# Attention values by key block in 64x64 quarters, and a Newton chain in PSUM

## The chip, the cores and the metric

The kernel runs on one core of a Trainium2 chip. The core has a matrix engine, TensorE (PE), whose weight loads are listed as PEld; VectorE (DVE), ScalarE (ACT) and GpSimd (POOL) for elementwise work; and SyncE (SP), which issues most transfers. SBUF and PSUM are its on-chip memories of 128 partitions. PE writes its results into PSUM, which has eight banks of 512 fp32 columns per partition. The metric is device time in microseconds (us) of one execution, the median of several runs.

## The reference

A windowed causal attention is followed by a gated expert. With 8 batches, 8 heads, 576 positions and 64 values per head:

```python
scores = scale * np.matmul(q, k.transpose(0, 1, 3, 2))
mask = (rel >= 0) & (rel < window)                 # window 64
attn = np.exp(scores - max); attn = attn / (sum + 1e-09)
out = np.matmul(attn, v)                           # (B, H, S, D)

x = out.transpose(0, 2, 1, 3).reshape(B * S, H * D)     # 4608 tokens of 512
xn = x / sqrt(mean(x * x) + 1e-06) * rms_g
g, val = xn @ w_gate, xn @ w_val                   # 512 x 1536
y = (g * sigmoid(g) * val) @ w_out                 # 1536 x 512
```

With a window of 64, a query sees only keys of its own block of 64 and of the block before it. So a key block j takes part in query blocks j and j+1 alone.

## The kernel before

**Batches, pairs, blocks.** Attention works on a pair of heads at a time: four pairs per batch, `n = 4 * b + hp`, 32 in all, each with nine blocks of 64 positions (`NBLK`). The expert works on nine tiles of 512 tokens: it takes its input as a high and a low half in fp16, and each product is three matmuls. Tiles 1 and 2 are done with plain products (`group_in`, `chunk_out`); tiles 3 to 8 with seven products on quarters of the operands instead of eight (`seventh`, L1213, and for the second layer `outer_unit`, L1093), whose weights are prepared beforehand (`prepare`, `prepare_out`) and loaded again from memory as `sevens` and `outer`. PE's unit of such a product is 12 matmuls of 128x256.

**An order written by hand.** After the start (batches 0 and 1, the widening of the weights, tile 0), `rest_of_tiles` (L1285) goes through slots. A slot is about one unit of PE (plain groups count two). `at_slot` enters a piece of work with a due time in slots, and all that is due by a slot is written into the program before the slot's unit. Each engine runs its instructions in this order. The due times of attention are in `WHEN` (one table for batches 2 and 3, one for 4 to 7), counted from the start of tile b - 1: `tile_start` gives 0, 72 and 144 for batches 2, 3 and 4, then 63 more for each. `PREPARE` and `PREPARE_OUT` hold start and spacing of the preparations.

**Banks.** In this stage all eight banks of PSUM go through one list (`any_bank`, L97): the first of the list is taken, and `done_with` puts a bank at its end when the last reader has been written into the program. PE waits on the chip until that reader has run. In tiles 3 to 8 a product a1 keeps its bank over the units 0 to 12 of its chunk, a5 from unit 2 to 8, a2 for one unit; chunks start seven slots apart; `times` (L1169 to L1173) frees a bank some two to three slots after its last unit (`DONE`, `TANH`, `TIMES`). Scores take three banks: s0 for block 0, then one for each head; the masks free s0 first.

**Attention of a pair in batches 2 to 7.** `load_kv` (L340) loads keys and values in one transfer. The values lie with even blocks in partitions 0 to 63 and odd blocks in 64 to 127; `even` holds block 2u above block 2u - 1. A query block j needs key blocks j - 1 and j under one another: for even j that is not what `even` has, so two further transfers (L363, L364) load a shifted copy, `odd`. `scores_of_pair` (L430) multiplies queries by keys in quarters (`quarter`, L408): 64 rows of one head, 64 columns of one block, up to 128 keys; the four (head, parity) quarters follow one another in the order of `QUARTERS`. The mask (DVE, L425), exponential (ACT, L428) and scaling (POOL, L383) follow; then the weights are turned by a way through memory (L391, L397) and a transpose of 32x32 blocks (DVE, L400, L401). `values` (L606) then does `attention_values` (L536) in two halves of five and four query blocks, the second half due 0.4 slot after the first: for each block and head one matmul of 128 rows (two key blocks), 64 columns and 64 queries into a bank `xp`, and one copy by ACT (L623) into `xb`. `squares` (ACT) and `add` (POOL, for the last pair DVE, L647) collect the sum of squares. They are due 1.5 and 2.2 slots after the values, and use the pair's keys as scratch.

**Roots.** `inverse_roots` (L765) sums the squares over partitions with matmuls into a bank `tot` (five columns) and `inverse_root` (L783) makes 1/sqrt from them on DVE: a line into m (L785), a first guess from the bits of m (L786), then three Newton steps of three instructions (L790 to L792) on the SBUF tile `rm` (m, r, w). `broadcast` (L794) spreads r with matmuls (`rb`, L801), and `normalise` scales and halves the tile's input.

Of the kernel before, what the change touches and what calls it, by code (L numbers as in the profile page):

```python
# [15 lines left out]
F32 = mybir.dt.float32  # L16
# [6 lines left out]
ALU = mybir.AluOpType  # L23
# [20 lines left out]
WHEN = [{'scores': [-13.59, -5.21, 8, 18.26], 'values': [15.58, 22.47, 33.48, 46.85], 'queries': [-6, -6, -6, -6], 'keys': [-6.13, -8.13, -6, -5.32], 'turn': [23.21, 22, 22, 22.22], 'back': [15.94, 16, 16, 15.39], 'away': [12.41, 12.5, 12.08, 13.25], 'mask': [0.36, 0.57], 'exp': [1.39, 0.67], 'sum': 9.7, 'scale': 10, 'roots': 50.0, 'first': [52.21, 0.85], 'second': [58.92, 1.15]}, {'scores': [-15.06, -4.11, 7.56, 21.23], 'values': [16.7, 22, 34.61, 46.18], 'queries': [-4.86, -8.35, -5.85, -6], 'keys': [-6, -6, -5.27, -6], 'turn': [20.48, 23.66, 23.92, 21.6], 'back': [16, 16, 16, 15.9], 'away': [12.5, 12.5, 11.38, 12.5], 'mask': [0.38, 0.71], 'exp': [1.49, 0.69], 'sum': 9.7, 'scale': 10, 'roots': 50.5, 'first': [53.82, 0.85], 'second': [59.57, 0.85]}]  # L44
# [5 lines left out]
PREPARE_OUT = [(117.64, 0.7), (127.0, 0.7), (135.37, 0.7), (145.0, 0.7), (154.0, 0.7), (163.0, 0.7)]  # L50
HALVES = 0.4
DONE = 1.05
TANH = 0.88
# [1 line left out]
SUMS_AT = 0.78  # L55
FREED = 1.1
STREAM = (20, 38)
PREPARE = [(3.0, 0.9), (11.29, 0.9), (23.04, 0.9), (31.8, 1.05), (41.96, 1.07), (51.0, 0.9), (60.6, 0.77), (69.87, 0.9), (79.8, 1.08), (87.32, 0.8), (99.16, 1.41), (113.5, 1.05)]
ST = 2 * NBLK * P - 32
NRB = B  # L60
S1 = [-2, 1, 3, 6, 10, 12.5, 15.5, 19]
# [12 lines left out]
def tile_window_attention_moe(  # L74
# [265 lines left out]
    def load_kv(n):  # L340

        if n == 3:
            kvt = wk.tile([P, 2, NKD, TT], F16, tag="xn", name=f"kv_{n}")
            kvt = kvt.rearrange("p a b c -> p (a b c)").bitcast(F32)[:, : S + NBLK * P]
        else:
            kvt = wk.tile([P, S + NBLK * P], F32, tag="kv", name=f"kv_{n}", bufs=NKV)
        if n < NPAIR:
            nc.sync.dma_start(out=kvt[:, :S], in_=kv[n, :, :S])
        else:
            nc.sync.dma_start(out=kvt[:, : S + NKT * P], in_=kv[n])  # L350
        even = kvt[:, S : S + NKT * P].rearrange("p (u c) -> p u c", c=P)
        odd = kvt[:, S + NKT * P :].rearrange("p (u c) -> p u c", c=P)

        def values_in():
            nc.sync.dma_start(out=kvt[:, S : S + NKT * P], in_=kv[n, :, S : S + NKT * P])
            nc.vector.tensor_copy(odd[0:D], even[0:D, : NKT - 1, :])
            nc.vector.tensor_copy(odd[D:P], even[D:P, 1:, :])

        if n < NPAIR:
            later[n] = values_in  # L360
        else:
            src = kv[n, :, S : S + NKT * P].rearrange("p (u c) -> p u c", c=P)
# [42 lines left out]
    def units(g, h):  # L405
        return [1 + 4 * g + 2 * h + i for i in range(2)] + ([0] if g == h == 0 else [])
# [110 lines left out]
    def weights_to_keys(n, g, ps):  # L517
# [15 lines left out]
            pts.append(pt)  # L533
        return pts

    def attention_values(n, g, at, vv, xp):  # L536

        xp = xp or x_bank(f"xp_{n}_{g}")
        for c, j in enumerate(range(5) if g == 0 else range(5, 9)):
            rows = slice(0, P if j else D)  # L540
            for h in range(2):
                hd = slice(h * D, (h + 1) * D)
                i, par = divmod(j - 1 - 4 * g, 2)
                w = at(1 + 4 * g + 2 * h + i, rows, par) if j else at(0, rows, h)
                o = xp[hd, c * D : (c + 1) * D]
                nc.tensor.matmul(  # L546
                    o if len(w.shape) == 2 else o.rearrange("p (a b) -> p a b", b=32),
                    lhsT=vv[j][rows, hd],
                    rhs=w,
                    start=True,  # L550
                    stop=True,
                    skip_group_check=True,
                )
        return xp
# [3 lines left out]
    def attention(b):  # L558
# [21 lines left out]
        def moves(hp):  # L580
            n = b * NPAIR + hp

            def turned():
                p, m, _ = whole.pop(n)
                turn(p, m)
                soft[hp, 0] = soft[hp, 1] = p
# [15 lines left out]

        def to_keys(hp, g):
            soft[hp, g] = weights_to_keys(b * NPAIR + hp, g, soft[hp, g])

        def values(hp, g, xp=None):  # L606
            n = b * NPAIR + hp
            assert b < TB or chain[n] == 4 + g
            chain[n] = 5 + g
            vv = pairs[hp][1]  # L610
            p = soft.pop((hp, g))
            if isinstance(p, list):
                place = {u: p[h][:, i, :] for h in range(2) for i, u in enumerate(units(g, h))}
                at = lambda u, rows, a: place[u][rows, a * D : (a + 1) * D]
            else:
                at = lambda u, rows, a: p[rows, 2 * a : 2 * a + 2, slot(u), :]
# [24 lines left out]
        def add(hp):  # L641
            ssq = norm["ssq"]
            chain["add", b] = chain.get(("add", b), 0) + 1
            assert chain[b * NPAIR + hp] == 6 and chain["squares", b] >= chain["add", b]
            if hp:
                e = nc.vector if (E('ADD', 'ppvppv')[3 * b + hp - 1] == 'v' if b < 2 else hp == NPAIR - 1) else nc.gpsimd
                e.tensor_tensor(ssq, ssq, pairs[hp][0], ALU.add)  # L647
# [10 lines left out]
            return normalise(b, norm["x"], norm["r"], piece)  # L658

        if b >= TB:  # L660
            return load_queries, load_keys, score_pair, moves, values, squares, add, roots, normal_parts
        return load_queries, load_keys, score, to_keys, values, roots, normal

    def attention_events(b, start, pace, tags):
# [25 lines left out]
            timed.sort(key=lambda e: e[:2])  # L690

    def attention_slots(b):
        load_queries, load_keys, score_pair, moves, values, squares, add, roots, normal_parts = attention(b)
        t0 = tile_start(b - 1)

        def all_of(hp, when):
# [11 lines left out]
        for hp in range(NPAIR):  # L708
# [74 lines left out]
    def inverse_root(m, r, w, squares):  # L783
# [3 lines left out]
            r.bitcast(I32), m.bitcast(I32), -0.5, RSQRT_SEED, ALU.mult, ALU.add  # L787
        )
        for _ in range(3):
            nc.vector.tensor_tensor(w, r, r, ALU.mult)  # L790
            nc.vector.scalar_tensor_tensor(w, w, -0.5, m, ALU.mult, ALU.mult)
            nc.vector.scalar_tensor_tensor(r, w, 1.5, r, ALU.add, ALU.mult)  # L792

    def broadcast(b, r, a, z):  # L794
# [722 lines left out]
```

## Time and profile before

| what | value |
|---|---|
| runs | 991.19, 991.77, 991.29 us; median 991.29 |
| profiled execution | 990.32 us, its span 988.5 |
| granted PE clock, mean of the span | 0.983 |
| moved by DMA | 193.89 MB, mean 196 GB/s |
| instructions | 22548 |

The profile is of one execution. It has the busy time of each engine, groups of instructions by line, what ended the idle time before an instruction (in brackets, with an arrow to the engine, tile and line it waited for), a timeline, and windows with busy time, granted PE clock (1.00 is full) and DMA share. A row of the timeline is start, length, engine, line, operation, output and inputs, shape and how many were merged. A fp32 matmul appears as two records. PE's records overlap at their ends, since matmuls are pipelined, so the cost of a piece on PE is better read from one start to the next. In rows of waits the numbers are the sum in us, how often, and the longest.

### The profile page before, as it was taken

To read this page: it belongs to the slowest core of one execution; us is meant where nothing else is said; L and a number is where in the kernel's file an instruction comes from. 1 tells how busy PE (TensorE), PEld (TensorE's weight loads), DVE (VectorE), ACT (ScalarE), POOL (GpSimd) and SP (SyncE) were. 2 spreads that over 40 slices of the span, in tenths; PEclk is the share of its full clock that TensorE was granted. 3 is DMA by queue.
4 is the path that set the end of the run, shared out by engine and by line. 5 is a ranking of instruction groups with operands and counts; after the bars stand their busy time and mean duration, and the time that the engine had idled before them with its cause. 6 is when DMAs were issued, how large, how long until landed. Compare 5 with 4: busy or idle time off the path is not lost.

```text
span 988.5 us, 22548 instructions
## 1 busy us (share of the span) xinstructions
PE 950.5 (96%) x8465; PEld 693.4 (70%) x8465; DVE 663.8 (67%) x1839; ACT 545.6 (55%) x1404; POOL 420.3 (43%) x481
## 2 busy tenths in 40 slices
PE   7779989999999999989999999999999999999998
PEld 5544544544444454467888888888888898888887
DVE  5678968248776766869865776778577846743761
ACT  5567887245435543356755674676477536642652
POOL 3335643134424542344635454545345525440440
PEclk9989989999999999999999999999999999999999
DMA  7525661226545875477758976887598736645641
GB/s 289 188 86 183 208 216 37 70 86 181 132 132 162 220 222 171 140 240 265 228 212 255 326 241 206 288 295 263 187 299 299 224 103 231 203 143 194 223 156 43
DMA packets 106653, 193.89 MB, mean 196 GB/s; under 512 B 28208, under 2 KB 65072, under 8 KB 106544
## 3 DMA queue, kind: packets, MB, share of 16 engines
q1 hardware_dynamic: 105968, 191.27, 60.7%
q8 instruction: 66, 1.08, 0.4%
q10 hardware_dynamic: 576, 1.18, 0.3%
q14 instruction: 43, 0.35, 0.1%
HBM read 154.67 MB, written 37.75 MB: 195 GB/s over the span
## 4 chain that ended last, share of the span: by engine, by line
PE 88%; DMA 4%; DVE 4%; ACT 3%; issue 1%; SPq 1%; ACTq 0%; DVEq 0%
PE a L1141 32%; PE o L1084 15%; PE xp L546 5%; PE sc L412 4%; PE pv L888 3%; PE po L888 3%; PE po L890 3%; PE pg L888 3%; PE po L889 3%; PE pv L890 3%; PE pv L889 3%; PE pg L890 3%; PE pg L889 3%; DMA kv<-kv 2%; DMA wt<-sevens 1%; PE tr L527 1%
## 5 line engine op out<-in xcount | busy, mean ns | idle before, releaser
L1141 PEld LDWEIGHTS <-wt 128*128 128x128 f16 x3024 | 294.2, 98 | 37.9 <-issue 0.8
L1141 PE MATMUL a<-xn,wt 128*128 128x256 f16 x1728 | 203.1, 273 | 0.0
L1210 POOL TENSOR_TENSOR wt<-u,wt 128x512 f16<-128x512 f32 x72 | 66.2, 920 | 152.6 <-ACT wt L1208 98.6
L1141 PE MATMUL a<-wt,wt 128*128 128x256 f16 x1044 | 127.1, 273 | 0.0
L1175 ACT ACTIVATE th<-a,hsc 128x256 f32<-128x256 f32 x144 | 67.9, 472 | 94.4 <-DVE a L1239 75.7
L1210 POOL TENSOR_TENSOR h<-th,h 128x512 f16<-128x512 f32 x72 | 85.5, 1189 | 45.8 <-ACT h L1208 44.1
L1084 PE MATMUL o<-wt,h 128*128 128x256 f16 x864 | 101.1, 273 | 0.0
L428 ACT ACTIVATE pm<-pm,st 128x128 f32<-128x128 f32 (+1 forms) x216 | 83.8, 390 | 19.7 <-DVE st L425 19.5
L1084 PEld LDWEIGHTS <-h 128*128 128x128 f16 x864 | 84.1, 98 | 10.6 <-issue 1.0
L1170 DVE SCALAR_TENSOR_TENSOR th<-th,a 128x256 f32<-128x256 f32 x144 | 59.4, 412 | 34.5 <-ACT th L1175 32.7
L1239 DVE TENSOR_TENSOR a<-a,s 128x512 f32<-128x512 f32 x72 | 50.2, 697 | 46.1 <-PE a L1141 43.6
L383 POOL TENSOR_TENSOR pm<-pm,st 128x512 f32<-128x512 f32 (+1 forms) x72 | 60.5, 866 | 41.9 <-DVE st L461 20.5
L1084 PEld LDWEIGHTS <-wt 128*128 128x128 f16 x648 | 63.5, 99 | 7.2
L941 POOL TENSOR_TENSOR h<-th,h 128x512 f16<-128x512 f32 x30 | 38.2, 1273 | 65.2 <-ACT h L940 55.4
L1171 DVE SCALAR_TENSOR_TENSOR th<-a,th 128x256 f32<-128x256 f32 x144 | 61.1, 424 | 5.0
L412 PE MATMUL sc<-kv,q 64*64 64x128 f32 (+1 forms) x1056 | 55.7, 297 | 8.3 <-DMA q<-q 4.9
L425 DVE CUSTOM_DVE_ANT_0 pm<-sc,blocked 128x128 f32<-128x128 f32 x192 | 49.3, 283 | 15.4 <-PE sc L412 15.3
L888 PE MATMUL pg<-xn,wt 128*128 128x512 f16 x144 | 55.0, 382 | 2.3 <-ACT wt L249 1.5
L888 PE MATMUL pv<-xn,wt 128*128 128x512 f16 x144 | 55.8, 388 | 0.7 <-DVE th L936 0.7
L890 PE MATMUL pv<-xn,wt 128*128 128x512 f16 x144 | 55.9, 388 | 0.0
L889 PE MATMUL pv<-xn,wt 128*128 128x512 f16 x144 | 55.8, 387 | 0.0
L888 PEld LDWEIGHTS <-wt 128*128 128x128 f16 x296 | 29.2, 99 | 36.8 <-issue 2.4
(197 smaller groups left out, 1940.1 us busy)
## 6 DMA issues: line engine op xcount, KB each, us to landing
wt<-sevens SPq DMA_DIRECT2D x72, 512.0 KB, 5.3
wt<-sevens SPq DMA_DIRECT2D x36, 768.0 KB, 5.0
wt<-outer SPq DMA_DIRECT2D x24, 768.0 KB, 4.5
kv<-kv SPq DMA_DIRECT2D x28, 608.0 KB, 5.5
via<-pm SPq DMA_DIRECT2D x96, 144.0 KB, 3.4
pm<-via SPq DMA_DIRECT2D x24, 576.0 KB, 4.4
q<-q SPq DMA_DIRECT2D x28, 288.0 KB, 5.1
kv<-kv SPq DMA_DIRECT2D x56, 128.0 KB, 6.0
```

The source lines that it names most:

```text
L383: nc.gpsimd.tensor_tensor(p[:, :ks, us, :], p[:, :ks, us, :], r, ALU.mult)
L412: nc.tensor.matmul(out.rearrange("p (n c) -> p n c", c=D), lhsT=qt[hd, j * D : (j + 1) * D], rhs=halves[hd, :1, :] if j == 0 else halves[h ...
L428: nc.scalar.activation(part, part, AF.Exp, bias=low, scale=-1.0, accum_out=total)
L888: nc.tensor.matmul(acc, lhsT=lh, rhs=rh, start=first, stop=False)
L889: nc.tensor.matmul(acc, lhsT=lh, rhs=rl, start=False, stop=False)
L890: nc.tensor.matmul(acc, lhsT=ll, rhs=rh, start=False, stop=last)
L1084: nc.tensor.matmul(acc[:, sub * HT : (sub + 1) * HT], lhsT=l[:, x, sub * P : (sub + 1) * P], rhs=r[:, y, :], start=first and c == cs[0] an ...
L1141: nc.tensor.matmul(acc[:, i * HT : (i + 1) * HT], lhsT=ws[l][:, kt, :], rhs=b[:, m, kt, :], start=at_start, stop=kt == 1 and j == 2, skip_ ...
L1170: nc.vector.scalar_tensor_tensor(cols, cols, 1.0, acc[:, :HT], ALU.add, ALU.mult)
L1171: nc.vector.scalar_tensor_tensor(cols, acc[:, HT:], 2.0**-42, cols, ALU.mult, ALU.mult)
L1175: nc.scalar.activation(cols, acc[:, :HT], AF.Tanh, scale=th_scale[:, c : c + 1])
L1210: nc.gpsimd.tensor_tensor(lo, src, hi, ALU.subtract)
```

## The change

For pairs of batches 2 to 7 values are computed by key block. Key block m (64 rows: the lower or upper half of the partitions by its parity) is multiplied by the weights of query blocks m and m + 1 at once, for each head: sixteen matmuls of 64 rows, 64 columns and 128 queries and two of 64 queries (block 8), in the order of `QUARTERS`. Even and odd key blocks go to separate banks: x0 has query blocks 0 to 5 of the even ones, x1 blocks 6 to 8, x2 blocks 1 to 8 of the odd ones. The three banks are taken together. `take` copies x0 and x1 (ACT, 384 and 192 columns) and adds x2 (DVE, 512 columns), 0.9, 1.0 and 1.3 slots after the values; squares and additions follow at 2.2 and 3. The shifted copy is no longer loaded for these pairs. The weights are in one tile for the whole pair, as before.

In the roots, m and w are now columns of the bank `tot`, which is released after the chain; the Newton step multiplies m by r first, then by r again. This holds for all eight batches.

Due times change too (before, after):

| entry | before | after |
|---|---|---|
| batches 2 and 3, values | 15.58, 22.47, 33.48, 46.85 | 12.69, 20.07, 33.48, 43.56 |
| back | 15.94, 16, 16, 15.39 | 16.42, 16.48, 16.48, 15.87 |
| away, third pair | 12.08 | 13.8 |
| exp, sum, scale | 1.39, 9.7, 10 | 1.34, 10.6, 10.9 |
| roots; first piece | 50.0; 52.21 by 0.85 | 50.9; 54.11 by 0.93 |
| batches 4 to 7, scores, third pair | 7.56 | 7.51 |
| values, fourth pair | 46.18 | 46.28 |
| turn, second pair | 23.66 | 23.78 |
| first piece; second piece | 53.82; 59.57 | 54.15; 57.1 |
| PREPARE, 1st; 6th; 7th; 8th | 3.0; 51.0 by 0.9; by 0.77; by 0.9 | 2.8; 51.89 by 1.11; by 0.98; by 0.88 |
| PREPARE_OUT, 5th | 154.0 by 0.7 | 154.12 by 0.82 |

```diff
+TAKEN = [0.9, 1.0, 1.3]
+SQUARED = [2.2, 3]
...
         if n < NPAIR:
             later[n] = values_in
-        else:
+        elif n < TB * NPAIR:
             src = kv[n, :, S : S + NKT * P].rearrange("p (u c) -> p u c", c=P)
             nc.sync.dma_start(out=odd[0:D], in_=src[0:D, : NKT - 1, :])
             nc.sync.dma_start(out=odd[D:P], in_=src[D:P, 1:, :])
+        else:
+            return kvt[:, :S], [even[(j % 2) * D : (j % 2 + 1) * D, (j + 1) // 2, :] for j in range(NBLK)]
...
+    def values_by_keys(n, p, vv):
+
+        xs = [x_bank(f"x{i}_{n}") for i in range(3)]
+
+        def product(m, h):
+            x, j0 = (xs[2], 1) if m % 2 else (xs[0], 0) if m < 6 else (xs[1], 6)
+            rows, hd = slice((m % 2) * D, (m % 2 + 1) * D), slice(h * D, (h + 1) * D)
+            js = range(m, min(m + 2, NBLK))
+            w = []
+            for j in js:
+                i, par = divmod(j - 1, 2)
+                u, a = (1 + 4 * (i // 2) + 2 * h + i % 2, par) if j else (0, h)
+                w.append(p[rows, 2 * a : 2 * a + 2, slot(u), :])
+            step = w[-1].offset - w[0].offset
+            nc.tensor.matmul(
+                x[hd, (m - j0) * D : (m - j0 + len(w)) * D].rearrange("p (x a b) -> p x a b", x=len(w), b=32),
+                lhsT=vv[m][:, hd],
+                rhs=bass.AP(tensor=p.tensor, offset=w[0].offset, ap=[w[0].ap[0], [step, len(w)], *w[0].ap[1:]]),
+                start=True,
+                stop=True,
+                skip_group_check=True,
+            )
+
+        for m in range(0, NBLK - 1, 2):
+            for h, odd in QUARTERS:
+                product(m + odd, h)
+        for h in range(2):
+            product(NBLK - 1, h)
+        return xs
...
+        def weigh_values(hp):
+            n = b * NPAIR + hp
+            sums[hp] = values_by_keys(n, soft.pop((hp, 0)), pairs[hp][1])
+
+        def take(hp, i):
+            n = b * NPAIR + hp
+            if hp == i == 0:
+                new_sums()
+            x = norm["x"][:, hp, :]
+            if i < 2:
+                a, z = ((0, 6 * D), (6 * D, S))[i]
+                nc.scalar.copy(x[:, a:z], sums[hp][i][:, : z - a])
+            else:
+                nc.vector.tensor_tensor(x[:, D:], x[:, D:], sums[hp][i], ALU.add)
+            done_with(f"x{i}_{n}")
...
-            at_slot(v, partial(values, hp, 0))
-            at_slot(v + 0.4, partial(values, hp, 1))
-            at_slot(v + 1.5, partial(squares, hp))
-            at_slot(v + 2.2, partial(add, hp))
+            at_slot(v, partial(weigh_values, hp))
+            for i in range(3):
+                at_slot(v + TAKEN[i], partial(take, hp, i))
+            at_slot(v + SQUARED[0], partial(squares, hp))
+            at_slot(v + SQUARED[1], partial(add, hp))
...
-        rm = wk.tile([P, 3, nst], F32, tag="rm", name=f"rm_{b}", bufs=1)
-        m, r, w = (rm[:, i, :] for i in range(3))
+        r = wk.tile([P, nst], F32, tag="rm", name=f"rm_{b}", bufs=1)
+        m, w = (tot[:, 8 * i : 8 * i + nst] for i in range(1, 3))
...
         for _ in range(3):
-            nc.vector.tensor_tensor(w, r, r, ALU.mult)
-            nc.vector.scalar_tensor_tensor(w, w, -0.5, m, ALU.mult, ALU.mult)
+            nc.vector.tensor_tensor(w, m, r, ALU.mult)
+            nc.vector.scalar_tensor_tensor(w, w, -0.5, r, ALU.mult, ALU.mult)
             nc.vector.scalar_tensor_tensor(r, w, 1.5, r, ALU.add, ALU.mult)
```

More of the change, by code (lines that the diff above doesn't have):

```diff
@@ L43 @@
 LV0 = [2.6, 2.6, 2.6, 2.6, 2.6, 2.6, 2.6, 2.6]
-WHEN = [{'scores': [-13.59, -5.21, 8, 18.26], 'values': [15.58, 22.47, 33.48, 46.85], 'queries': [-6, -6, -6, -6], 'keys': [-6.13, -8.13, -6, -5.32], 'turn': [23.21, 22, 22, 22.22], 'back': [15.94, 16, 16, 15.39], 'away': [12.41, 12.5, 12.08, 13.25], 'mask': [0.36, 0.57], 'exp': [1.39, 0.67], 'sum': 9.7, 'scale': 10, 'roots': 50.0, 'first': [52.21, 0.85], 'second': [58.92, 1.15]}, {'scores': [-15.06, -4.11, 7.56, 21.23], 'values': [16.7, 22, 34.61, 46.18], 'queries': [-4.86, -8.35, -5.85, -6], 'keys': [-6, -6, -5.27, -6], 'turn': [20.48, 23.66, 23.92, 21.6], 'back': [16, 16, 16, 15.9], 'away': [12.5, 12.5, 11.38, 12.5], 'mask': [0.38, 0.71], 'exp': [1.49, 0.69], 'sum': 9.7, 'scale': 10, 'roots': 50.5, 'first': [53.82, 0.85], 'second': [59.57, 0.85]}]
+WHEN = [{'scores': [-13.59, -5.21, 8, 18.26], 'values': [12.69, 20.07, 33.48, 43.56], 'queries': [-6, -6, -6, -6], 'keys': [-6.13, -8.13, -6, -5.32], 'turn': [23.21, 22, 22, 22.22], 'back': [16.42, 16.48, 16.48, 15.87], 'away': [12.41, 12.5, 13.8, 13.25], 'mask': [0.36, 0.57], 'exp': [1.34, 0.67], 'sum': 10.6, 'scale': 10.9, 'roots': 50.9, 'first': [54.11, 0.93], 'second': [58.92, 1.15]}, {'scores': [-15.06, -4.11, 7.51, 21.23], 'values': [16.7, 22, 34.61, 46.28], 'queries': [-4.86, -8.35, -5.85, -6], 'keys': [-6, -6, -5.27, -6], 'turn': [20.48, 23.78, 23.92, 21.6], 'back': [16, 16, 16, 15.9], 'away': [12.5, 12.5, 11.38, 12.5], 'mask': [0.38, 0.71], 'exp': [1.49, 0.69], 'sum': 9.7, 'scale': 10, 'roots': 50.5, 'first': [54.15, 0.85], 'second': [57.1, 0.85]}]
 FIRST7 = 3
@@ L49 @@
 OUT_ORDER = ((1, 0), (1, 1), (5, 0), (5, 1), (2, 0), (2, 1), (1, 2), (5, 2)) + tuple((p, u) for p in (6, 3, 7) for u in range(3)) + ((2, 2), (4, 0), (4, 1), (4, 2))
-PREPARE_OUT = [(117.64, 0.7), (127.0, 0.7), (135.37, 0.7), (145.0, 0.7), (154.0, 0.7), (163.0, 0.7)]
+PREPARE_OUT = [(117.64, 0.7), (127.0, 0.7), (135.37, 0.7), (145.0, 0.7), (154.12, 0.82), (163.0, 0.7)]
+TAKEN = [0.9, 1.0, 1.3]
+SQUARED = [2.2, 3]
 HALVES = 0.4
@@ L57 @@
 STREAM = (20, 38)
-PREPARE = [(3.0, 0.9), (11.29, 0.9), (23.04, 0.9), (31.8, 1.05), (41.96, 1.07), (51.0, 0.9), (60.6, 0.77), (69.87, 0.9), (79.8, 1.08), (87.32, 0.8), (99.16, 1.41), (113.5, 1.05)]
+PREPARE = [(2.8, 0.9), (11.29, 0.9), (23.04, 0.9), (31.8, 1.05), (41.96, 1.07), (51.89, 1.11), (60.6, 0.98), (69.87, 0.88), (79.8, 1.08), (87.32, 0.8), (99.16, 1.41), (113.5, 1.05)]
 ST = 2 * NBLK * P - 32
@@ L585, in turned @@
                 turn(p, m)
-                soft[hp, 0] = soft[hp, 1] = p
+                soft[hp, 0] = p
             when = WHEN[b > FIRST7]
@@ L604, in to_keys, with new_sums @@
             soft[hp, g] = weights_to_keys(b * NPAIR + hp, g, soft[hp, g])
+        sums = {}
+        def new_sums():
+            norm["x"] = wk.tile([P, NPAIR, S], F32, tag="xb", name=f"xb_{b}", bufs=1)
+            norm["ssq"] = wk.tile([P, S], F32, tag="ssq", name=f"ssq_{b}", bufs=1)
+        def weigh_values(hp):
+            n = b * NPAIR + hp
+            assert chain[n] == 4
+            chain[n] = 5
+            sums[hp] = values_by_keys(n, soft.pop((hp, 0)), pairs[hp][1])
+        def take(hp, i):
+            n = b * NPAIR + hp
+            assert chain[n] == 5 + i
+            chain[n] = 6 + i
+            if hp == i == 0:
[7 more added lines that the diff above has]
+            done_with(f"x{i}_{n}")
         def values(hp, g, xp=None):
             n = b * NPAIR + hp
-            assert b < TB or chain[n] == 4 + g
-            chain[n] = 5 + g
             vv = pairs[hp][1]
             p = soft.pop((hp, g))
[L612 to L616, printed above, removed]
+            place = {u: p[h][:, i, :] for h in range(2) for i, u in enumerate(units(g, h))}
+            at = lambda u, rows, a: place[u][rows, a * D : (a + 1) * D]
             xp = attention_values(n, g, at, vv, xp)
             if hp == g == 0:
-                norm["x"] = wk.tile([P, NPAIR, S], F32, tag="xb", name=f"xb_{b}", bufs=1)
-                norm["ssq"] = wk.tile([P, S], F32, tag="ssq", name=f"ssq_{b}", bufs=1)
+                new_sums()
             xb, ssq = norm["x"], norm["ssq"]
@@ L624, in values @@
             done_with(f"xp_{n}_{g}")
-            if g == 0:
-                return
-            if b < TB:
+            if g:
                 squares(hp)
@@ L643, in add @@
             chain["add", b] = chain.get(("add", b), 0) + 1
-            assert chain[b * NPAIR + hp] == 6 and chain["squares", b] >= chain["add", b]
+            assert (b < TB or chain[b * NPAIR + hp] == 8) and chain["squares", b] >= chain["add", b]
             if hp:
@@ L660, in attention @@
         if b >= TB:
-            return load_queries, load_keys, score_pair, moves, values, squares, add, roots, normal_parts
+            return load_queries, load_keys, score_pair, moves, weigh_values, take, squares, add, roots, normal_parts
         return load_queries, load_keys, score, to_keys, values, roots, normal
@@ L692, in attention_slots @@
     def attention_slots(b):
-        load_queries, load_keys, score_pair, moves, values, squares, add, roots, normal_parts = attention(b)
+        load_queries, load_keys, score_pair, moves, weigh_values, take, squares, add, roots, normal_parts = attention(b)
         t0 = tile_start(b - 1)
```

## The prediction

> **What bounds the kernel now.** I read the page first, then what TensorE (PE) waits for once the attention of batch 2 has begun, then PE's timeline piece by piece.
>
> ```profile
> PE 950.5 (96%) x8465; PEld 693.4 (70%) x8465; DVE 663.8 (67%) x1839; ACT 545.6 (55%) x1404; POOL 420.3 (43%) x481
> ```
>
> PE is busy for 96% of the span and no other engine for more than 67%. The second view groups PE's waits from 220 us to the end: total, number, longest.
>
> ```profile
> PE s L412 <- DMA kv<-kv: 2.9, 2, 2.5
> PE tot L769 <- DVE ssq L647: 2.6, 2, 2.1
> PE xp L546 <- DVE th L1171: 2.3, 1, 2.3
> ```
>
> That is 7.8 us of waiting in 768 us. So in this stage the time is what PE's own pieces cost, and an edit counts if it shortens a piece, removes one of these three waits, or makes a new one. The reader should see that the first wait is for keys and the other two are for VectorE (DVE).
>
> The profiled execution took 990.32 us (span 988.5); the median of the runs is 991.29. I sum against 990.32 and add the 0.97 at the end.
>
> **Values: what a pair costs now, and in quarters.** Rows of PE's timeline: start, length, line, shape, count.
>
> ```profile
> 503.33 1.41 PE L546 MATMUL xp<-pm,kv 64*64 64x64 f32 x36
> 504.67 1.48 PE L1141 MATMUL a<-xn,wt 128*128 128x256 f16 x12
> 506.09 0.27 PE L412 MATMUL s<-kv,q 64*64 64x64 f32 x2
> ...
> 507.23 0.94 PE L1084 MATMUL o<-wt,h 128*128 128x256 f16 x7
> ```
>
> Lengths overlap by a tail, so the cost of a piece is the difference of two starts. A pair's values in one go cost 504.67 - 503.33 = 1.34. A pair's scores cost 507.23 - 506.09 = 1.14. Both are 36 records (18 fp32 matmuls, two records each). The scores are sixteen matmuls of 64x64x128 and two of 64x64x64 over the four quarters of the array, with banks separated by the row half; the new values are the same sixteen and two, also with a bank for each row half. So I price the new values at the scores' row: 1.14. Their right side comes in runs of 32 floats where the scores' comes in runs of 64; the values' runs are of 32 today too.
>
> In batches 4 to 7 most pairs are not in one go: the second half is due 0.4 slot after the first, and where a slot begins between them a product unit comes in between.
>
> ```profile
> 532.85 1.47 PE L1141 MATMUL a<-wt,wt 128*128 128x256 f16 x12
> 534.16 1.47 PE L1141 MATMUL a<-xn,wt 128*128 128x256 f16 x12
> ...
> 554.40 0.95 PE L546 MATMUL xp<-pm,kv 64*64 64x64 f32 x20
> 555.28 1.48 PE L1141 MATMUL a<-xn,wt 128*128 128x256 f16 x12
> 556.70 0.69 PE L546 MATMUL xp<-pm,kv 128*64 128x64 f32 x16
> 557.31 0.39 PE L1141 MATMUL a<-wt,wt 128*128 128x256 f16 x2
> ```
>
> The two halves cost 0.88 and 0.61. The unit between them takes 1.42, an ordinary one 1.31 (534.16 - 532.85): going over to fp32 costs 0.11 each time. A split pair therefore pays 0.88 + 0.61 + 0.11 = 1.60 where a pair in one go pays 1.34, and saves 0.46; a pair in one go saves 0.20. By the due times (16.7 and 17.1, 22 and 22.4, 34.61 and 35.01 are split; 46.18 and 46.58 not) each of batches 4 to 7 has three split pairs and one whole. In batches 2 and 3 a slot in which this matters is two units long or the pair lies inside one, and all eight are whole. The group is 864 records, that is 24 pairs:
>
> ```profile
> L546 PE MATMUL xp<-pm,kv x864: 216/222/366, 233.3 to 793.0; 128*64 128x64 f32 x154, 64*64 64x64 f32 x19
> ```
>
> Batches 2 and 3: 8 x 0.20 = 1.6. Batches 5 to 7: 3 x (3 x 0.46 + 0.20) = 4.7. Batch 4: its last two pairs 0.46 + 0.20 = 0.7; its first two go into the fourth term. **First term: -7.0.** Bounds: 0 if quarters of values run no faster than the present row; nothing in the trace shows a form faster than the scores'.
>
> **Roots of batches 2 and 3.** There the values of the last pair were due at 46.85, squares and addition up to 2.2 later (49.05), roots at 50.0. Now they are due at 43.56, 46.56 and 50.9: 4.3 slots of room in place of 0.95.
>
> ```profile
> 393.53 1.28 PE L769 MATMUL tot<-one,ssq 128*128 128x1 f32 x10 [2.09 <-DVE ssq L647]
> 395.00:399.00 4.00, 4.00 (x13) 1.43 (x11) 3.39 (x13) 0.00 (x0) 0.72 (x1) 0.57 0.21 66
> 467.00:471.00 4.00, 4.00 (x35) 2.86 (x33) 3.90 (x17) 2.91 (x8) 2.29 (x3) 0.57 0.80 271
> ```
>
> The bracket is PE's wait. In the windows the number before the last two is the granted clock: after this wait of 2.09 us PE had 0.57 of its clock for 4 us, a loss of 4 x 0.43 = 1.72. Room of 4.3 slots (a slot is the 1.31 above) is more than both waits, so I take them as gone: 2.6 + 1.7. **Second term: -4.3**; bounds -2.6 (the clock dips anyway) and -4.3. In batches 4 to 7 the room shrinks, from 2.1 slots to 1.2, and I see no wait there yet.
>
> **Roots' chain in PSUM.** Start, length, engine:
>
> ```profile
> 50.19 2.13 POOL L244 TENSOR_TENSOR wt<-wt 128x1024 f16<-128x1024 f32 x1 [0.51 <-ACT wt L243]
> 50.37 1.97 DVE L786 TENSOR_SCALAR rm<-rm 128x5 int32<-128x5 int32 x1
> 54.28 0.55 PE L801 MATMUL rb<-ident,rm 128*128 128x128 f32 x1 [4.14 <-DVE rm L792]
> 394.56 1.15 POOL L999 TENSOR_TENSOR lo<-r,hi 128x512 f16<-128x512 f32 x1
> 394.84 0.17 DVE L785 TENSOR_SCALAR rm<-tot 128x5 f32<-128x5 f32 x1 [1.37 <-PE tot L769]
> 395.04 0.70 DVE L786 TENSOR_SCALAR rm<-rm 128x5 int32<-128x5 int32 x1
> 395.78 0.16 DVE L790 TENSOR_TENSOR rm<-rm 128x5 f32<-128x5 f32 x1
> ```
>
> L786 works on five columns, yet it took 1.97 us in batch 0 and ended with GpSimd's (POOL's) instruction; in batch 3 it took 0.70 and again ended with POOL's. L785, the same kind of instruction but reading PSUM, ran in 0.17 inside that same POOL instruction. After the change L786 reads PSUM, so I give it 0.17: 1.80 saved in batch 0, where PE stands 4.14 us for this chain. What follows it up to 60 us hangs on the same chain, so nearly all should stay. Small results written to PSUM are shown nowhere (L1239 below writes 512 columns there in 0.70); 0.2 is kept back for them. **Third term: -1.6**; bounds 0 and -1.8. Elsewhere the chain is covered: the rows of L801 wait nowhere else. [...]
>
> **The third bank, at the second pair of batches 4 to 7.** Values take three banks at once where they took one. Banks go round first in, first out. At slot t0+22 (t0 = 144 for batch 4) five of eight are held: two a1, one a5, and the two score banks of the last pair. Free are three: one that a2 left (due 163.95), one that a1 left (165.07) and s0, whose reader, the mask of the same slot's scores, is due at 165.61. The odd blocks' bank is the third popped and the second that PE writes. So values now stand behind that mask and all that DVE has before it; and PE being in order, the products of slot 166 and after stand behind values.
>
> ```profile
> 563.04 0.23 DVE L425 CUSTOM_DVE_ANT_0 pm<-s,blocked 128x64 f32<-128x64 f32 x1
> 563.61 0.57 PE L546 MATMUL xp<-pm,kv 64*64 64x64 f32 x6
> 457.50 0.42 DVE L1170 SCALAR_TENSOR_TENSOR th<-th,a 128x256 f32<-128x256 f32 x1 [0.27 <-ACT th L1175]
> 463.12 1.48 DVE L1019 TENSOR_TENSOR ro<-wt 128x512 f32<-128x512 f16 x1 [0.58 <-DMA outer<-hi_o]
> 465.53 1.04 PE L546 MATMUL xp<-pm,kv 64*64 64x64 f32 x20 [2.26 <-DVE th L1171]
> 468.27 0.22 DVE L425 CUSTOM_DVE_ANT_0 pm<-s,blocked 128x64 f32<-128x64 f32 x1
> 469.59 0.82 PE L1141 MATMUL a<-wt,wt 128*128 128x256 f16 x3
> ```
>
> In batch 5 the mask ends at 563.27, 0.34 before values start: no wait. In batch 4, which alone has the last preparation of the outer weights (L1019) beside it, DVE is behind; values waited 2.26 for a2's bank and the mask came only at 468.27. DVE waited nowhere between 457.50 and there but for 0.58. The change puts a DVE addition of 128x512 into this stretch, due at 162.0:
>
> ```profile
> L1239 DVE TENSOR_TENSOR a<-a,s 128x512 f32<-128x512 f32 x72 | 50.2, 697 | 46.1 <-PE a L1141 43.6
> ```
>
> So the mask ends at 468.27 + 0.70 - 0.58 + 0.22 = 468.6 (I count the DMA wait as gone, since two issues are no longer ahead of it). From there: values 1.14, a unit 1.42, halved clock 1.72: 472.9. Before, the same point is 469.59; its pieces took 4.06 for 2.91 at full clock, so 0.57 of the 1.72 was still to come: 470.2. **Fourth term: +2.7**, the savings of these two pairs within it. Bounds: -0.9 (no new wait, two splits saved) and +4.
>
> **The rest, at nothing.** DVE's other 23 additions (0.70 each, 16 us in all) have its idle third for cover; the two ScalarE (ACT) copies carry the same 576 columns as before. The copies of the values go:
>
> ```profile
> kv<-kv SPq DMA_DIRECT2D x56, 128.0 KB, 6.0
> SPq L350 <- PE xp L546: 45.4, 9, 16.7
> ```
>
> 48 of 56 vanish. They come after the keys' transfer in the queue, and of the waits quoted first those for kv are for keys, so their going moves none of them; the 2.5 us in batch 4 stay. SyncE's queue (SP) stands, in the second row, for values that still read the buffer which the next kv load wants; values now end as early or earlier, so what is queued behind that load (weights, the outer blocks) comes earlier. Squares and additions of batches 4 to 7 end 0.8 slot later and release the same buffers, but the next load into such a buffer is due 15 slots later or more.
>
> **Sum:** -7.0 - 4.3 - 1.6 + 2.7 = -10.2, so 980.1 against 990.32, and 981.1 on the scale of the medians.
>
> **Rivals.**
> 1. No new wait in batch 4: DVE reaches the mask sooner, or another bank is free. Then the fourth term is -0.9: 977.5. For it: preparation of the fifth outer block is respaced just before. Against: DVE has no idle time to give.
> 2. Values do not gain from quarters. Then the first term is 0: 988.1. For it: four streams with rows cut in 32s are shown nowhere. Against: the scores' row.
> 3. Emptying binds a little everywhere: three reads per pair, and values, ACT and DVE each late by some 0.2 us per pair, 24 x 0.2 = 4.8: 985.9. For it: after values the next product takes a bank released 0.1 slot earlier. Against: ACT is 55% busy.
> 4. Slower. The wait behind the mask of s0, in batches 5 to 7 too. The room there is 0.34. If DVE came 3 us late, PE would stand 2.7 and lose 1.7 of clock: 3 x 4.4 = 13.2, 994.3. It decides from some 2.6 us of lateness on (3 x 4.0 cancels the gain). Against: DVE was not late there in any batch before, and additions are due 2 slots off or more. [...]
>
> **How the numbers follow.** Forecast 0.62 (981.1; alone 979 to 984, by the bounds of the last three terms). Rival 1: 0.15. Rival 3: 0.10. Rival 2: 0.08. Rival 4: 0.05. Range 976.5 to 986.5, which leaves out rivals 2 and 4 and the edges. A measurement of this kernel tells about 0.2%, 2 us, from no change. Rival 2 ends 3.2 below 991.29, but half of it reaches into the band; so faster 0.91, same 0.04, slower 0.05.
>
> **What would show it.** Right: pieces of 36 records at L546's successor costing about 1.14; no wait of tot in batches 2 and 3; L786 near 0.17 in batch 0 and PE's wait for rb near 2.3; in batch 4 a single wait of five to six us for DVE's mask. Wrong: pieces of 1.3 or more, waits for banks in batches 5 to 7, or PE idle at new places before 220 us.

## The result, and the profile after

| | before | after |
|---|---|---|
| runs | 991.19, 991.77, 991.29, 987.98 | 978.50, 978.46, 976.07, 979.91 |
| median, us | 991.24 | 978.48 |
| profiled execution, its span | 990.32, 988.5 | 978.5, 976.7 |
| ratio of the times | | 0.9876 (95%: 0.9847 to 0.9905) |

The change makes the kernel 1.24% faster (0.95 to 1.53). 978.48 stands against a forecast of 981.1 and a range of 976.5 to 986.5.

The busy line of the page after:

```profile
PE 939.3 (96%) x8454; PEld 689.7 (71%) x8465; DVE 681.3 (70%) x1863; ACT 546.8 (56%) x1404; POOL 420.2 (43%) x481
```

PE is busy 11.2 us less, DVE 17.5 more (mostly the additions of the odd blocks), and the bound is the same as before: PE. What PE waits for from 220 us on, in the same view as before:

```profile
PE x L554 <- DVE st L429: 2.8, 1, 2.8
PE x L554 <- DVE th L1224: 1.9, 1, 1.9
PE s L416 <- DVE t L936: 1.7, 1, 1.7
PE s L416 <- DMA kv<-kv: 1.2, 1, 1.2
PE s L416 <- DVE th L1223: 0.3, 1, 0.3
```

These sum to 7.9 us where 7.8 were waited before, but they are other waits. Those of the roots (`tot`) are gone. The new values, L554, wait twice in batch 4. The rest stands before scores. The third row, at 534 us in batch 5, names a DVE instruction, but that one works on SBUF alone and frees no bank. The wait is most likely about keys too: their load was issued at 528.15 and landed 5.6 later, 0.25 before PE went on.

**Values.** Two pairs of batch 5, the first whole, the second split before the change (start, length):

```profile
547.03 1.22 PE L554 MATMUL x<-pm,kv 64*64 64x128 f32 x36
548.18 1.49 PE L1194 MATMUL a<-xn,wt 128*128 128x256 f16 x12
...
555.79 1.24 PE L554 MATMUL x<-pm,kv 64*64 64x128 f32 x36
556.96 1.49 PE L1194 MATMUL a<-wt 128*128 128x256 f16 x12
```

From start to start 1.15 and 1.17. All 23 pairs without a wait cost 1.15 to 1.17; 1.14 was the row of the scores.

**The roots of batch 0.** The same three instructions as before, under their new lines:

```profile
50.26 2.13 POOL L246 TENSOR_TENSOR wt<-wt 128x1024 f16<-128x1024 f32 x1 [0.50 <-ACT wt L245]
...
50.45 0.16 DVE L839 TENSOR_SCALAR rm<-tot 128x5 int32<-128x5 int32 x1
...
52.58 2.05 PE L854 MATMUL rb<-ident,rm 128*128 128x128 f32 x8 [2.38 <-DVE rm L845]
```

L839 is the former L786. It runs in 0.16 inside POOL's instruction, where it took 1.97 and ended with it. PE's wait is 2.38 in place of 4.14.

**Where the time went.** A pair's first scores matmul is the same piece in both programs, so the difference of its starts is what had been gained by then. Before, then after (the one at 506.09 of before stands in the prediction):

```profile
161.92 0.33 PE L412 MATMUL s<-kv,q 64*64 64x64 f32 x4 [1.76 <-DVE st L425]
...
406.12 0.27 PE L412 MATMUL s<-kv,q 64*64 64x64 f32 x2
...
439.12 0.33 PE L412 MATMUL s<-kv,q 64*64 64x64 f32 x4 [2.54 <-DMA kv<-kv]
...
462.06 0.27 PE L412 MATMUL s<-kv,q 64*64 64x64 f32 x2
```

```profile
160.51 0.33 PE L416 MATMUL s<-kv,q 64*64 64x64 f32 x4 [1.76 <-DVE st L429]
...
398.34 0.27 PE L416 MATMUL s<-kv,q 64*64 64x64 f32 x2
...
429.97 0.33 PE L416 MATMUL s<-kv,q 64*64 64x64 f32 x4 [1.17 <-DMA kv<-kv]
...
450.84 0.27 PE L416 MATMUL s<-kv,q 64*64 64x64 f32 x2
...
497.54 0.27 PE L416 MATMUL s<-kv,q 64*64 64x64 f32 x2
```

| stretch of before, us | gained | forecast for it | what differs |
|---|---|---|---|
| to 161.92 | 1.41 | 1.6 | seven halved windows of the clock in both traces |
| to 406.12 (batches 2, 3) | 6.37 | 5.9 (eight pairs 1.6, roots 4.3) | |
| to 439.12 | 1.37 | 0 | the wait for keys, 2.54, became 1.17 |
| to 462.06 (first values of batch 4) | 2.07 | 0.46 | 1.6 from a clock that was not halved behind that wait |
| to 506.09 (the other three) | -2.67 | -2.5 (0.66 and a stall of 3.16) | |
| to the end | 3.25 | 4.7 | scores of batch 5 waited 1.68 where it was 0.40, and of batch 7 0.25 |
| sum | 11.80 | 10.2 | |

Every row comes out near its term when the waits before scores are set aside, and these make up the difference: 1.4 + 1.6 - 1.5 = 1.5 of the 1.6 us.

### The profile page after: what moved, and what is told of

Read it like the earlier page. It is cut to its first block, busy times and chain, and to the rows that moved or that the text cites. A ratio compares the mean times of both kernels' runs of the same rounds, so it can differ in the third digit from the quotient of the medians.

```text
span 976.7 us, 22491 instructions
## 1 busy us (share of the span) xinstructions
PE 939.3 (96%) x8454; PEld 689.7 (71%) x8465; DVE 681.3 (70%) x1863; ACT 546.8 (56%) x1404; POOL 420.2 (43%) x481
## 4 chain that ended last, share of the span: by engine, by line
PE 90%; DMA 4%; ACT 3%; DVE 2%; issue 1%; SPq 0%; DVEq 0%; ACTq 0%
PE a L1194 32%; PE o L1137 16%; PE sc L416 4%; PE po L941 3%; PE pv L941 3%; PE po L943 3%; PE pg L941 3%; PE po L942 3%; PE pv L942 3%; PE pv L943 3%; PE pg L943 3%; PE pg L942 3%; PE x L554 3%; DMA kv<-kv 2%; PE xp L580 1%; PE tr L531 1%
## 5 line engine op out<-in xcount | busy, mean ns | idle before, releaser
L1194 PEld LDWEIGHTS <-wt 128*128 128x128 f16 x3024 | 294.9, 98 | 36.9 <-issue 0.5
L1137 PEld LDWEIGHTS <-h 128*128 128x128 f16 x864 | 84.1, 98 | 10.6 <-issue 1.0
L1137 PEld LDWEIGHTS <-wt 128*128 128x128 f16 x648 | 63.4, 98 | 7.2
L1224 DVE SCALAR_TENSOR_TENSOR th<-a,th 128x256 f32<-128x256 f32 x144 | 61.1, 424 | 4.9
L882 DVE SCALAR_TENSOR_TENSOR xb<-xb,gsb,rb 128x384 f32<-128x384 f32 (+7 forms) x64 | 30.5, 508 | 36.8 <-PE rb L854 36.7
```

The source lines that it names most:

```text
L1137: nc.tensor.matmul(acc[:, sub * HT : (sub + 1) * HT], lhsT=l[:, x, sub * P : (sub + 1) * P], rhs=r[:, y, :], start=first and c == cs[0] an ...
L1194: nc.tensor.matmul(acc[:, i * HT : (i + 1) * HT], lhsT=ws[l][:, kt, :], rhs=b[:, m, kt, :], start=at_start, stop=kt == 1 and j == 2, skip_ ...
L1224: nc.vector.scalar_tensor_tensor(cols, acc[:, HT:], 2.0**-42, cols, ALU.mult, ALU.mult)
```

## The experiments

Each was run beside the kernel before on the same chip. Ratios are to that kernel, whose medians there were 988.98 to 990.69, with 95% intervals. The theory is the prediction's: quarters for values, room before the roots, a small chain freed from POOL, and one loss, in batch 4, where values stand behind DVE. The rivals are its rivals, and for the waits for keys that the two unread copies had delayed them.

**Only the roots' due time (on the kernel before).** Batches 2 and 3 alone:

```diff
-'roots': 50.0, 'first': [52.21, 0.85]
+'roots': 52.0, 'first': [54.21, 0.85]
```

> The kernel before with the roots of batches 2 and 3 due at 52.0 in place of 50.0 and the first piece at 54.21 in place of 52.21, nothing else. My theory: both waits for the sum of squares go (0.5 and 2.1), and the halved clock behind the second with them (1.7): 4.3 less, 986.9. Rival: the clock dips there anyway, for another reason; then 2.6 less, 988.6. [...]

984.05 (8 runs), ratio 0.9952 (0.9936 to 0.9968): 4.7 us less. In its trace the scores at 406.12 of before come 4.76 sooner. The first scores of batch 2 start at 161.92 in both traces, so all 4.76 are this edit's, against 4.3. Its waits from 220 us on:

```profile
PE s L412 <- DMA kv<-kv: 5.3, 3, 2.8
PE xp L546 <- DVE th L1171: 2.3, 1, 2.3
```

`tot` is gone from the list. Two due times moved by two slots, and nothing else, give over a third of what the whole change gives. It has nothing to do with quarters.

**Only the roots' chain in PSUM (on the kernel before).** With it goes the new order of the products, as in the change:

```diff
-        rm = wk.tile([P, 3, nst], F32, tag="rm", ...)
-        m, r, w = (rm[:, i, :] for i in range(3))
+        r = wk.tile([P, nst], F32, tag="rm", ...)
+        m, w = (tot[:, 8 * i : 8 * i + nst] for i in range(1, 3))
```

> The kernel before with the roots' chain alone as in the change (m and w in the bank of the sums, the new order of the products). My theory: L786 in batch 0 goes from 1.97 to 0.17 us, PE's wait for rb from 4.14 to about 2.4, and about 1.5 of it stay to the end: 989.7. Rival: the start has cover, and the gain is eaten by waits up to 220 us: 991.2.

987.85 (10 runs), ratio 0.9995 (0.9981 to 1.0008). The interval holds both no change and the 1.5 that was expected, so the times settle nothing. The trace shows the mechanism itself:

```profile
49.25 0.17 DVE L786 TENSOR_SCALAR rm<-tot 128x5 int32<-128x5 int32 x1
...
51.39 2.04 PE L801 MATMUL rb<-ident,rm 128*128 128x128 f32 x8 [2.38 <-DVE rm L792]
```

The wait is 2.38 against 4.14, as in the full change. Why 1.76 at this place doesn't show in ten runs is seen in the last section: up to 165 us executions of one kernel differ by more, and this trace, 4.68 ahead of before's at the scores of 161.92, owes most of that to chance.

**Only the split taken away (on the kernel before).** Values in the old form, both halves due together:

```diff
-            at_slot(v + 0.4, partial(values, hp, 1))
+            at_slot(v, partial(values, hp, 1))
```

> The kernel before with the second half of a pair's values due together with the first (0 in place of 0.4 slot later), so that no product unit comes between. My theory: the split costs 0.26 us in each of 12 pairs, 3.1 in all, of which batch 4's second pair may lose part since its second bank comes late: 2.5 to 3.1 less, 988.4. Rival: the gain of the change's values is the quarters' alone; then 991.2, no change.

987.23 (10 runs), ratio 0.9982 (0.9968 to 0.9996), 1.8 us less where 2.5 to 3.1 were expected. Every pair without a wait costs 1.34 to 1.38 in its trace, so the 0.26 of a split is real. Part of it goes again: waits for keys of 0.73, 0.94 and 1.27 stand where 0.40 was waited, and in batch 4 two waits for DVE sum to 2.68 where there was one of 2.26:

```profile
464.15 1.04 PE L546 MATMUL xp<-pm,kv 64*64 64x64 f32 x20 [1.46 <-DVE th L1171]
466.41 1.10 PE L546 MATMUL xp<-pm,kv 128*64 128x64 f32 x16 [1.22 <-DVE th L1171]
```

This execution, the slowest of its ten, keeps nearly nothing: its span is 988.4 where before's was 988.5.

**The copies loaded all the same (on the changed kernel).** The shifted copy of the values is loaded for all pairs and read by nothing.

```diff
-        elif n < TB * NPAIR:
+        else:
             src = kv[n, :, S : S + NKT * P].rearrange("p (u c) -> p u c", c=P)
...
-        else:
+        if n >= TB * NPAIR:
```

> The changed kernel with the two 128 KB transfers of the shifted copy kept for batches 2 to 7 (nothing reads them). By the prediction they come behind the keys in the queue and matter for no wait: 978.5 within 1. Rival, from the profile after: they share the transfer engines with the keys; then the third pair of batch 4 waits for its keys 2.5 us again where it waited 1.17, the clock halves behind it (1.7), and the time rises by about 3, to 981.5.

977.90 (4 runs), ratio 0.9876 (0.9851 to 0.99), the same as without them. The waits for keys are as in the changed kernel (1.17 and 1.68 there):

```profile
429.71 0.33 PE L416 MATMUL s<-kv,q 64*64 64x64 f32 x4 [1.34 <-DMA kv<-kv]
...
533.43 0.27 PE L416 MATMUL s<-kv,q 64*64 64x64 f32 x2 [1.69 <-DMA kv<-kv]
```

So 6.3 MB less from memory bring nothing, as costed, and the shorter wait in batch 4 is not their doing.

**A second read of x2 (on the changed kernel).** One more DVE copy of 128x512 from the bank per pair, into unused space, before the bank goes back:

```diff
                 nc.vector.tensor_tensor(x[:, D:], x[:, D:], sums[hp][i], ALU.add)
+                nc.vector.tensor_copy(spare.pop(n), sums[hp][i])
             done_with(f"x{i}_{n}")
```

> The changed kernel with one more VectorE read of the odd blocks' bank per pair in batches 2 to 7, a copy of 128x512 into space of the kv tile that nothing reads (about 0.65 us each, 24 of them, 16 us in all). My theory: VectorE has cover everywhere but in front of the mask in batch 4, so the time rises by 0.7 to 1.5, to about 979.5. Rival: emptying PSUM binds in general; then most of the 16 us shows, 985 to 994.

977.85 (4 runs), ratio 0.9886 (0.9853 to 0.9919). The group of the copies, and all that PE waits for from 470 us to the end (batches 5 to 7):

```profile
L666 DVE COPY kv<-x 128x512 f32<-128x512 f32 x24 | 16.4, 683 | 0.0
```

```profile
PE s L418 <- DMA kv<-kv: 1.4, 2, 0.8
```

16.4 us more on DVE, and no wait for a bank in batches 5 to 7. Even the upper end of the interval, 0.9919, stays under the 985 us of this run's rival. Emptying does not bind here: rivals 3 and 4 fall.

**The last preparation of the outer weights later (on the changed kernel), twice.** If values in batch 4 stand behind a DVE that the preparation makes late, moving the preparation must free them:

```diff
-PREPARE_OUT = [..., (154.12, 0.82), (163.0, 0.7)]
+PREPARE_OUT = [..., (154.12, 0.82), (168.0, 0.7)]
```

> The changed kernel (978.5, profiled span 976.7) with the last preparation of the outer weights due at 168.0 in place of 163.0, behind the mask of s0 and the values of batch 4's second pair. My theory: that preparation is what VectorE has in front of the mask, and the mask frees the third bank; so both waits there (1.92 and 2.79 us) and the halved clock behind them (some 3 us) go, and the time falls by about 7.7, to 971. Rival: values there wait for something else, the turned weights or the values' transfer; then the time stays at 978.5 within 1.

972.21 (4 runs), ratio 0.9817 (0.9791 to 0.9844). Then again, with the changed kernel beside it on one chip:

> The changed kernel with the last preparation of the outer weights moved from slot 163 to 168, again, beside the changed kernel on one chip. In the first pair of traces the stall of batch 4's second pair was 5.9 us cheaper, but 2.3 us and a halved window had gone to keys before it, 2.1 to keys in batch 7, and 3.4 had come from fewer halved windows before 160 us. If those keys' waits are chance the difference of the two times is 5 to 6 us; if they belong to the earlier products, 2 to 4 us; under 2 us if the gain of 6 was the halved windows before 160 us alone.

> The changed kernel itself, on the same chip as the next one. Two things are asked. Time: about 0.988 of the kernel before. Clock: in the traces so far the halved clock comes in whole windows of 3.41 us whose starts lie on one grid of 3.41 us per execution, at another phase in each; so the waits of batch 4's second pair (1.9 and 2.8) should be there again, with one to three halved windows behind them, all halved stretches multiples of 3.41 us on one grid, and the number of those before 160 us between 4 and 7. Rival: the halving hangs on the wait itself (its length), then the stretches are where they were in the first trace, moved by the same amount as the waits.

972.57 (6 runs), ratio 0.9834 (0.9808 to 0.9859); the changed kernel 977.15 (5 runs), 0.9869 (0.9847 to 0.9892). The difference of 4.6 lies between the two answers that were given ahead. In its second trace the changed kernel has the two waits of its first again (1.6 and 2.8), with two halved windows behind them. The stall of the changed kernel, first PE, then DVE, then two windows (the clock is third from the end):

```profile
453.96 0.40 PE L554 MATMUL x<-pm,kv 64*64 64x128 f32 x2 [1.92 <-DVE th L1224]
457.15 2.26 PE L554 MATMUL x<-pm,kv 64*64 64x128 f32 x34 [2.79 <-DVE st L429]
459.35 2.74 PE L1194 MATMUL a<-t,wt 128*128 128x256 f16 x12
```

```profile
452.01 1.02 DVE L1072 TENSOR_TENSOR ro<-wt 128x512 f32<-128x512 f16 x1
...
456.87 0.22 DVE L429 CUSTOM_DVE_ANT_0 pm<-s,blocked 128x64 f32<-128x64 f32 x1
```

```profile
455.67:459.08 3.41, 1.93 (x33) 1.93 (x34) 3.31 (x11) 2.48 (x7) 2.11 (x2) 0.50 0.80 264
459.08:462.49 3.41, 3.41 (x20) 2.41 (x17) 0.89 (x4) 1.08 (x6) 0.97 (x2) 0.50 0.32 95
```

The first matmul needs the bank that a2 left; the second goes to x2 and starts 0.06 after the mask of s0 has ended (457.09). Then PE has half its clock for 6.8 us. With the preparation moved, all that PE waits for from 220 us on, in the second of the two traces:

```profile
PE s L416 <- DMA kv<-kv: 1.4, 1, 1.4
PE x L554 <- DVE st L429: 1.0, 1, 1.0
PE a L1194 <- DVE a L1292: 0.8, 1, 0.8
```

Between the scores at 422 and those at 506 of before this kernel gains 5.67 us on before and the changed kernel, in the trace beside it, 0.75: the stall and its halved clock cost 4.9. In the first of the two traces the gain of this stretch was 3.30, because the third pair's scores in it waited 2.21 in place of 1.40 and a halved window followed. (The row of that wait names a DVE instruction, L1224; in the second trace the same scores start ahead of it, so it was keys that held them.) And batch 7 had a wait for keys that the second trace has not:

```profile
739.21 0.27 PE L416 MATMUL s<-kv,q 64*64 64x64 f32 x2 [2.39 <-DMA kv<-kv]
```

So the waits for keys differ by up to 2.4 us between two executions of one program. Ten runs of this version lie between 969.78 and 975.85, nine of the changed kernel between 974.73 and 979.91. It is the fastest that was run.

**s0's bank to x1 (on the changed kernel).** The third bank popped goes to the product written from the 13th matmul on:

```diff
-        xs = [x_bank(f"x{i}_{n}") for i in range(3)]
+        xs = [x_bank(f"x{i}_{n}") for i in (0, 2, 1)]
+        xs = [xs[0], xs[2], xs[1]]
```

> The changed kernel with the third bank popped (s0's) given to x1, which PE writes from its 13th matmul on, in place of x2, which it writes second. Theory: in batch 4 the wait of 1.92 for the first banks stays, and the wait of 2.79 behind the mask moves to the 13th matmul and shrinks by twelve matmuls at the clock of the moment, 0.8 to 1.5 us: 977.0 to 977.7 on the scale of 978.5. Rival: it is not the mask of s0 that holds PE there; then the 2.8 stay at the second matmul and the time stays 978.5.

975.87 (4 runs), ratio 0.9849 (0.9829 to 0.9869), by the times not told from the changed kernel. In the trace:

```profile
452.81 0.40 PE L555 MATMUL x<-pm,kv 64*64 64x128 f32 x2 [1.55 <-DVE th L1225]
455.06 2.26 PE L555 MATMUL x<-pm,kv 64*64 64x128 f32 x34 [1.85 <-DVE th L1225]
```

From the first to the second matmul 2.25 where it was 3.19, so 0.94 is gained, within what was expected. The way is another: the wait did not move to the 13th matmul. The second now stands behind the next bank in the list, the one that a product a1 left, and by the time of the 13th the mask is done. That x2's matmul no longer waits for the mask shows that it was s0's bank that had held it.

**Keys of the third pair sooner (with the preparation moved), and this with the bank's order.**

```diff
-'queries': [-4.86, -8.35, -5.85, -6], 'keys': [-6, -6, -5.27, -6]
+'queries': [-4.86, -8.35, -6.8, -6], 'keys': [-6, -6, -6.7, -6]
```

> The kernel with the last preparation moved, and in it the third pair's keys and queries of batches 4 to 7 loaded 1.4 and 1 slots sooner, ahead of the returning weights (pm<-via) in SP's queue. Theory: what is left of the waits for keys is travel, 5.6 to 8.6 us on full DMA engines against a lead of some 5 us; issued 1.9 us sooner and ahead of 576 KB, the waits of 2.2 (with a halved window of 1.7 behind it), 0.3 and 2.4 us in batches 4, 5 and 7 go: 4.9 to 6.6 us, ratio to the kernel before 0.975 to 0.977. Rival: the weights' return is now the late one; DVE's transposes wait for it, a product bank behind them comes late, and PE waits as long for DVE: ratio as without, about 0.982.

> Last preparation moved, keys sooner and s0's bank given to x1, all three. Only some 1.0 us of waiting for banks is left there with the preparation moved, so the bank's order should bring at most 0.8 us beyond the kernel with the first two: ratio 0.974 to 0.977. Rival as for the keys alone: 0.982.

977.77 (5 runs), ratio 0.9866 (0.9846 to 0.9886), and 976.07 (5 runs), 0.9861 (0.9838 to 0.9885). No scores wait for keys any more in the first one's trace (that the wait in batch 7 is gone is not the edit's doing: it stood before the fourth pair), and yet, by the ratios, it is 3 to 5 us slower than without the edit. The bank's order on top of it makes no difference that the times tell. The rival came true, and more than it said. The weights' return is now issued behind the keys (at 421.93, they at 421.35), where it had gone ahead of them (421.58, 422.44), and DVE's transpose waits for it. Without the edit, in the second of the two traces, and with it:

```profile
425.93 1.25 DVE L404 STREAM_TRANSPOSE pm<-pm 128x1024 f32<-128x1024 f32 x1 [1.05 <-DMA pm<-via]
```

```profile
427.81 1.25 DVE L404 STREAM_TRANSPOSE pm<-pm 128x1024 f32<-128x1024 f32 x1 [2.67 <-DMA pm<-via]
```

And then PE waits:

```profile
446.22 4.09 PE L1194 MATMUL a<-xn,wt 128*128 128x256 f16 x36 [0.69 <-DVE a L1292]
...
452.66 0.40 PE L554 MATMUL x<-pm,kv 64*64 64x128 f32 x2 [1.21 <-DVE th L1224]
454.09 2.26 PE L554 MATMUL x<-pm,kv 64*64 64x128 f32 x34 [1.03 <-DVE st L429]
```

So DVE comes 1.6 us later to its work, and PE, without the wait of 1.40 for keys, sooner; PE waits for DVE at these places, and gets a halved window behind it. Which of the two moves costs more was not separated. From the scores at 422 to those at 506 of before it gains 2.50 us, against the 5.67 above. In batches 5 to 7 DVE stands 3.4 to 4.3 us before the same transpose, where it stood 1.0 to 1.5 without the edit, and waits for the mask of 0.42 and 0.45 come in batches 5 and 7. What else there may be of the difference was not followed further.

## Why the prediction was right

**Values in quarters, -7.0: right, in price and in count.** 1.15 to 1.17 was measured for the forecast 1.14, and the stretches where nothing else happens give the terms: 3.25 + 1.5 = 4.75 for batches 5 to 7 (4.7 forecast, the waits before scores set aside). The rows of 32 floats, on which rival 2 stood, cost nothing. Not all of the term is the quarters': ten splits at 0.26 are 2.6 of it, and values in the old form, in one go, save these too, less the waits that the experiment above shows.

**Roots of batches 2 and 3, -4.3: right.** The due times alone gave 4.76 in the trace; with 1.6 for the eight pairs that is the 6.37 of the table. So the term was a little small. The bound of -2.6, that the clock dips anyway, did not come in: no window between 166 and 455 us is halved after the change.

**The chain in PSUM, -1.6: right in the trace, too small for the times.** The wait fell by 1.76, and 1.41 was gained by the scores of batch 2, in two traces with seven halved windows each up to there. That both have seven is luck: by the last section traces with fewer gained up to 4.80 there. The nine small operations of the Newton steps take 0.16 to 0.17 each with m and w in PSUM, as they did on SBUF.

**The third bank, +2.7: right in size and place, in its form only half.** The mask ended at 457.09; with the 11.22 gained by then that is 468.3 on the scale of before, 468.6 was forecast. The stall cost 2.67 + 0.66 = 3.33, less the first pair's 0.46 2.87. But one wait of five to six us was forecast, and there are two, 1.92 for a2's bank as before and 2.79 for s0's, with two halved windows in place of one. Together these made 0.2.

**The rest, at nothing: the step that failed.** "The 2.5 us in batch 4 stay": they became 1.17, and the halved clock behind them went as well, together 3.0 gained. In return 1.5 were lost before scores of batches 5 and 7. The load's way from issue to landing took 8.1 us before and 5.8 after. The copies were rightly counted at nothing. Part of the difference is chance: the wait was 1.17, 1.52, 2.21 and 1.40 in four executions whose programs are the same up to this point. But not all: in the seven traces with the new values and the old due time of keys it is 1.17 to 2.21 and the load's way 5.8 to 6.9, in the four with the old values 2.09 to 2.83 and 7.6 to 8.3. So part goes with the change. With the copies loaded all the same the way was 6.2, so it is not they; what it is, stays open.

**The rivals.** Rival 1 fell with the stall (it would have been 977.5, close to the 978.5 that came about in another way), 2 with the 1.15, 3 and 4 with the second read of x2. (Rival 4 put the lateness that cancels the gain at 2.6 us. By its own terms it is 2.0, since 3 x 3.4 is already the gain of 10.2.) The forecast's own band, 979 to 984, was missed by 0.5. That the total came out so near owes something to gains and losses before scores that offset each other and that no term had. The median lies 2.6 under the forecast: 1.6 from the span, as the table shows, and 1.0 because the profiled execution of after stands at its median, where that of before was 0.97 under the one shown then.

## What to carry to other kernels

Look up in the trace what a form of matmul costs where it already runs, and price the new form at that row, from start to start. When a kernel in which one engine is 96% busy gets shorter pieces, ask at each place where that engine will now arrive sooner, and which engine or load it then waits for: here a load of keys moved ahead took away a wait of 1.4 us, but held up the load now behind it and with it DVE, and cost more than it saved. Before believing in a large edit, move only the due times: here 4.7 of 12 us were to be had by two numbers, and one more number gave 4.6 beyond the 12.

## What the runs showed of the hardware

PE's clock is halved in whole windows of 3.41 us on one grid per execution, and the grid begins anywhere: carried back to the start of the span, its first border lies 0.15 to 3.31 us after it. In the thirteen traces, cut on the grid of each, 103 of 3649 windows show a clock of 0.50, 3546 show 1.00, and none lies between. (The 1.00 of the first 33 us is doubtful: two records of `sc` took 0.69 us at 23.23 of before and 0.33 at 406.15, so PE seems to have run at half speed there.) From 200 us on the halving goes with how busy PE was in the window before, and so with how a wait lies on the grid, more than with its length: one of 2.54 us was followed by a halved window, one of 2.83 was not. Before, with a wait of 2.54 within one window (busy time of PE, and the clock third from the end):

```profile
436.50:439.91 3.41, 0.86 (x29) 0.82 (x32) 3.12 (x10) 0.35 (x1) 2.26 (x2) 1.00 1.00 285
439.91:443.32 3.41, 3.41 (x31) 2.32 (x22) 1.06 (x4) 1.43 (x6) 0.49 (x3) 0.50 1.07 372
```

and the kernel with the roots' due time alone, with a longer wait of 2.83 at the same scores that falls on the border of two windows:

```profile
429.34:432.75 3.41, 2.47 (x23) 1.96 (x21) 1.78 (x5) 1.44 (x4) 1.79 (x2) 1.00 1.04 307
432.75:436.17 3.42, 1.53 (x40) 1.35 (x41) 2.46 (x10) 1.29 (x4) 2.75 (x4) 1.00 1.02 295
436.17:439.58 3.41, 3.41 (x34) 3.06 (x32) 3.05 (x12) 1.86 (x7) 0.00 (x0) 1.00 1.05 366
```

Nothing is halved there. From 200 us on, the window after one at full clock was always halved when PE had been busy for less than 1.5 of the 3.41 us, never when for more than 2.05, and both happened between, so the busy time alone does not settle it there. So 1.7 us of a wait's price, half of 3.41, are a matter of where it falls. In the trace of before, waits of 2.1 to 2.5 us were enough, in windows in which PE was still busy for 0.86 to 2.01 us.

The executions of one kernel differ by this already ahead of batch 2. Gained on before's first trace at the first scores of batch 2, by the number of halved windows up to 165 us, for the nine traces of kernels with the new values: 7 windows 1.41, 1.65 and 1.83; 6 windows 2.48, 2.76, 3.02 and 3.45; 5 windows 3.95; 4 windows 4.80. Each window is worth about 1.1 us there, and the times of one kernel beside one another spread over up to 6.7 us. A gain of 1.76 in this stretch, as that of the roots' chain, was not to be told from nothing by ten runs.
